# Two sketch rows spread over heads by VectorE, and a task order searched with a price on tiling changes

## The chip, the cores and the metric

One core of a Trainium2 chip. The time of a kernel is the device time of one execution in microseconds (us), taken as the median of several executions. Executions come in a fast and a slow state, and only fast ones are compared; with one core, a run counts as slow when it is over 1.5% above the fastest of its kernel. "The profile" is one traced execution: its span is a little shorter than the timed figure (90.0 of 92.07 us before). TensorE appears as PE (matmuls) and PEld (weight loads), VectorE as DVE, ScalarE as ACT, GpSimd as POOL, SyncE as SP.

## The reference

Polynomial-sketch attention followed by an RWKV channel mix; everything is f32 at the interface.

```python
# q, k, v: [4 batches, 4 heads, 1088, 32];  S1, S2: [8, 32]
def phi(x):                                   # 64 features per token and head
    a = einsum('rd,bhsd->bhsr', S1, x); b = einsum('rd,bhsd->bhsr', S2, x)
    return einsum('bhsi,bhsj->bhsij', a, b).reshape(..., 64)
kv  = einsum('bhsf,bhsd->bhfd', phi(k), v);  z = phi(k).sum(axis=2)
x   = (phi(q) @ kv) / (phi(q) @ z + 1e-6)     # heads side by side: [4, 1088, 128]
# ... x_prev = x one token earlier; xk, xr = mixtures of x and x_prev by mu_k, mu_r
h   = max(xk @ w_k, 0);  v = (h * h) @ w_v    # w_k [128, 1024], w_v [1024, 128]
out = sigmoid(xr @ w_r) * v                   # [4, 1088, 128]
```

## The kernel before

The kernel is a list of tasks with an engine (and a PSUM bank) for each, written by a search that ran beforehand. The list fixes the order of instructions on every engine.

```python
ORDER = """
SS/PE/b0 SM/DVE SC3/ACT SC1/POOL ... KP0_0/PE/b0 KE0_0/ACT ... Z/5 KA0_0_0/PE/b0 ...
"""                                  # [cut] some 580 entries
for t, eng in plan.order(ORDER):
    dummy(t) if eng == "Z" else t["fn"](eng)
```

Names in it: KT/KP/KE/KF/KA are, for a batch's keys, transpose, projection, eviction, outer product and accumulation; KZ to KB fold the result; QT/Q1/.../QX are the same for groups of queries, up to the matmul that makes x; M1 and M2 are the two layers of the channel mix for a tile of 512 tokens (four blocks of 128), RE and SQ its relu and square, RR and SG its gate, FN the last multiply and OD the stores of an output tile.

The sketch rows are repeated over the four heads by the load itself, transposed on TensorE and then masked into block form:

```python
S8 = const.tile([R, 2, H, D], F32)                       # R = 8, H = 4, D = 32
load_k(0, nc.sync)
nc.scalar.dma_start(S8[:, 0], _ap(S1, [[0, H], [1, D]]))  # 32 runs of 128 bytes
nc.scalar.dma_start(S8[:, 1], _ap(S2, [[0, H], [1, D]]))
# ... [cut]
def s_rep():
    p = bank("ss")
    for x in range(2):
        nc.tensor.transpose(p[:, x * R:x * R + R], S8[:, x].rearrange("r h d -> r (h d)"), ident[:R, :R])
```

The key projection consists of short matmuls, two to a group of 128 tokens, each on half of the array (the tiling 128x64). The key accumulation is on quarters (128x32), the channel mix on the whole array (128x128).

```python
def k_proj(b, gi):
    t0, t1 = KG[gi]; p = bank(f"kab_{b}_{gi}")
    for t in range(t0, t1):
        for c in range(2):
            nc.tensor.matmul(p[64*c:64*c+64, (t-t0)*64:(t-t0)*64+64], kT[b][:, t, 64*c:64*c+64],
                             SW[:, 0, :H, :2, :], skip_group_check=True, tile_position=(0, 64*c))
```

Of the kernel before, what the change touches and what calls it, by code (L numbers as in the profile page):

```python
# [13 lines left out]
F32 = mybir.dt.float32  # L14
# [14 lines left out]
SS/PE/b0 SM/DVE SC3/ACT SC1/POOL SF/ACT SC2/POOL Z/2 S4T/PE/b0 KT0_0/DVE S4E/ACT KT0_1/DVE Z/2 KP0_0/PE/b0 KE0_0/ACT  # L29
KP0_1/PE/b1 KF0_0_1/POOL KF0_0_0/DVE KE0_1/ACT KF0_1_0/DVE KF0_1_1/POOL Z/5 KA0_0_0/PE/b0 KA0_0_1/PE WL/POOL  # L30
KA0_1_0/PE QT0_1/DVE KA0_1_1/PE MU/PE/b1 KC0/ACT KZ0/DVE QT0_0/DVE OM/ACT KD0/PE/b0 KG0/PE KW0/ACT KT1_0/DVE Q11/PE/b1
WRP/POOL Q10/PE/b2 KB0/DVE KT1_1/DVE QE1/ACT WRC/POOL KP1_0/PE/b0 QE0/ACT QP1/DVE Q12/PE/b3 QP0/DVE QD1/DVE KE1_0/ACT
QD0/DVE QI1/DVE QI0/DVE QN1/DVE KF1_0_0/POOL QN0/DVE QF1_0/DVE KP1_1/PE/b7 QE2/ACT KF1_0_1/DVE QR1_1/PE/b1 DL3k/DMA
QF0_0/POOL KE1_1/ACT QR1_0/PE/b4 QP2/DVE KA1_0_0/PE/b0 QV1_1/DVE QV1_0/ACT KF1_1_1/DVE KF1_1_0/POOL QR0_0/PE/b2
QD2/DVE QR0_1/PE/b4 QI2/DVE QV0_0/DVE QV0_1/ACT QT1_0/DVE QY0/PE/b4 QX1/PE/b2 QT1_1/DVE KA1_1_0/PE XL0/ACT XP0/ACT
XB0/DVE XF0/POOL XP1/ACT QN2/DVE KZ1/DVE DL3v/DMA KC1/ACT QF2_0/POOL XB1/ACT KD1/PE/b7 XK0/DVE KG1/PE XK1/DVE KW1/ACT
M10_1/PE/b4 M10_3/PE/b0 M10_0/PE/b1 KT2_1/DVE Q13/PE/b5 KB1/ACT QF2_1/POOL RE0_1/ACT DL3q/DMA RE0_3/ACT RE0_0/ACT
M11_2/PE/b4 KT2_0/DVE M11_4/PE/b0 M11_5/PE/b1 QE3/ACT M11_7/PE/b7 M11_6/PE/b2 RE1_4/ACT M11_0/PE/b6 SQ0_0/POOL QP3/DVE
RE1_5/ACT M11_3/PE/b3 RE1_2/DVE M10_4/PE/b0 RE1_0/ACT KP2_0/PE/b1 SQ1_2/POOL QD3/DVE RE1_6/ACT RE1_3/DVE RE0_4/ACT
RE1_7/ACT M20_0/PE/b6 QI3/DVE M10_5/PE/b2 M10_2/PE/b4 M10_7/PE/b0 SQ1_1/ACT QR2_1/PE/b3 QN3/DVE RE0_2/DVE QF3_0/DVE  # L40
QR2_0/PE/b7 RE0_7/ACT SQ0_1/POOL RE0_5/ACT QV2_1/ACT M11_1/PE/b0 QF3_1/DVE RR1/PE/b2 M10_6/PE/b4 RE1_1/ACT M20_1/PE
SG1/ACT RR0/PE/b3 QT2_1/DVE KP2_1/PE/b0 SQ1_0/POOL SQ1_3/ACT RE0_6/ACT QR3_0/PE/b2 KE2_0/ACT QT2_0/DVE QV2_0/ACT
QR3_1/PE/b4 SQ0_3/POOL KE2_1/DVE SQ0_2/ACT Q14/PE/b5 QV3_0/DVE KF2_0_1/POOL QV3_1/ACT KF2_1_1/DVE QY2/PE/b7 M20_2/PE
SG0/ACT M20_3/PE QX3/PE/b4 FN0/DVE KF2_0_0/POOL KT3_0/DVE OD0_0/DMA M21_0/PE/b6 QE4/DVE M21_1/PE XP2/ACT XB3/DVE
KF2_1_0/POOL M21_2/PE KA2_0_0/PE/b1 XB2/ACT XK2/DVE M21_3/PE RR2/PE/b3 XP3/DVE M12_0/PE/b7 M12_1/PE/b2 SG2/ACT
KA2_1_0/PE FN1/DVE XE0/POOL RE2_0/ACT KT3_1/DVE OD1_0/DMA M12_4/PE/b6 RE2_1/ACT M12_5/PE/b3 OD1_1/DMA M12_2/PE/b7
KC2/DVE RE2_4/ACT KZ2/DVE M12_6/PE/b0 RE2_5/DVE KD2/PE/b1 SQ2_0/ACT KG2/PE RE2_6/DVE SQ2_2/POOL M12_7/PE/b3
M12_3/PE/b6 KB2/DVE KP3_1/PE/b2 KW2/ACT QT3_1/DVE RE2_2/ACT Q15/PE/b1 RE2_3/ACT QP4/DVE RE2_7/ACT XL1/DVE Q16/PE/b6
QT3_0/DVE SQ2_1/ACT XF1/POOL QD4/DVE M22_0/PE/b3 QI4/DVE QN4/DVE KP3_0/PE/b7 SQ2_3/ACT XK3/DVE QF4_0/POOL M22_1/PE
KE3_0/DVE M22_2/PE QE5/ACT QF4_1/DVE QE6/ACT KF3_0_1/POOL M22_3/PE KE3_1/ACT QP5/DVE M13_1/PE/b4 KF3_0_0/DVE  # L50
M13_2/PE/b5 QR4_0/PE/b0 RE3_1/ACT KF3_1_0/POOL QD5/DVE FN2/DVE KA3_0_0/PE/b7 RE3_2/ACT QV4_0/ACT QI5/DVE M13_4/PE/b4
OD2_3/DMA KF3_1_1/DVE M13_0/PE/b5 QR4_1/PE/b3 OD2_1/DMA RE3_0/ACT QN5/DVE M13_3/PE/b0 QP6/DVE OD2_2/DMA QF5_0/POOL
QF5_1/DVE KA3_1_0/PE RE3_3/ACT OD2_0/DMA QV4_1/DVE M13_5/PE/b5 SQ3_1/ACT M13_7/PE/b0 SQ3_0/POOL M13_6/PE/b2 QD6/DVE
QR5_0/PE/b3 KZ3/DVE RE3_4/DVE QR5_1/PE/b1 KC3/ACT RE3_6/ACT QI6/DVE KD3/PE/b7 QY4/PE/b4 QN6/DVE QV5_0/ACT KG3/PE
QV5_1/DVE KW3/ACT RR3/PE/b2 RE3_5/ACT KB3/DVE QF6_1/POOL QF6_0/DVE QX5/PE/b1 RE3_7/ACT SQ3_2/ACT SQ3_3/POOL Q17/PE/b0
XP4/DVE XL2/ACT XB4/ACT QR6_1/PE/b6 XB5/DVE QE7/ACT RR4/PE/b5 SG3/ACT QP7/DVE Q18/PE/b7 XP5/ACT XK4/DVE XF2/POOL
M23_0/PE/b2 QD7/DVE SG4/ACT QV6_1/DVE XE1/POOL M14_7/PE/b4 M14_1/PE/b3 QI7/DVE M14_5/PE/b5 RE4_7/DVE M14_4/PE/b6
RE4_1/ACT M23_1/PE QN7/DVE RE4_4/ACT M14_0/PE/b4 RE4_5/DVE QF7_1/POOL M14_3/PE/b3 M23_2/PE RE4_0/ACT QF7_0/DVE
M14_2/PE/b5 SQ4_2/ACT M14_6/PE/b6 RE4_3/DVE SQ4_0/POOL QR6_0/PE/b4 QR7_0/PE/b0 QE8/DVE RE4_2/ACT QV6_0/DVE QR7_1/PE/b3
RE4_6/ACT Q19/PE/b5 QP8/DVE QV7_0/ACT XK5/DVE QY6/PE/b6 M23_3/PE QV7_1/ACT SQ4_1/POOL RR5/PE/b0 QE9/DVE SQ4_3/ACT  # L60
QD8/DVE QX7/PE/b3 FN3/DVE QI8/DVE SG5/ACT OD3_4/DMA QP9/DVE QN8/DVE M24_0/PE/b2 QD9/DVE OD3_3/DMA XL3/DVE XP6/ACT
QI9/DVE M15_1/PE/b0 XP7/DVE QF8_1/POOL OD3_0/DMA M15_3/PE/b1 XB6/ACT M24_1/PE OD3_1/DMA QN9/DVE RE5_3/ACT XB7/DVE
M24_2/PE OD3_2/DMA XE2/POOL RE5_1/ACT M24_3/PE QF9_0/DVE XF3/POOL M15_2/PE/b1 M15_7/PE/b0 QF8_0/POOL FN4/DVE
M15_4/PE/b4 RE5_2/ACT RR7/PE/b5 RE5_7/DVE RE5_4/ACT OD4_3/DMA QR9_1/PE/b2 M15_0/PE/b1 SQ5_1/POOL SG7/ACT XK7/DVE
OD4_1/DMA M15_6/PE/b4 QR8_0/PE/b0 RE5_0/ACT OD4_2/DMA RE5_6/DVE QR8_1/PE/b5 QV9_1/ACT OD4_0/DMA QV8_0/ACT QR9_0/PE/b1
XK6/DVE M15_5/PE/b2 SQ5_3/ACT RR6/PE/b4 QV8_1/DVE SQ5_0/POOL M17_5/PE/b6 M17_6/PE/b0 RE5_5/ACT M17_2/PE/b3 RE7_5/DVE
M17_0/PE/b5 QV9_0/ACT M17_7/PE/b7 RE7_6/DVE M17_3/PE/b2 RE7_2/ACT M17_1/PE/b6 QY8/PE/b1 RE7_3/ACT RE7_7/DVE
M17_4/PE/b3 M16_3/PE/b0 SG6/ACT SQ5_2/POOL RE7_0/DVE M16_5/PE/b2 M25_0/PE/b7 SQ7_1/ACT RE7_1/DVE M25_1/PE M16_6/PE/b5
RE7_4/DVE RE6_5/ACT M16_1/PE/b6 QX9/PE/b4 SQ7_0/ACT RE6_6/DVE SQ7_3/POOL RE6_1/DVE SQ7_2/ACT M25_2/PE XP9/DVE M25_3/PE
XB9/DVE RE6_3/ACT M16_4/PE/b6 XB8/DVE M16_0/PE/b5 M16_7/PE/b3 RE6_4/ACT M16_2/PE/b2 FN5/DVE XE3/POOL M27_0/PE/b0  # L70
RE6_0/ACT SQ6_2/POOL RE6_2/DVE M27_1/PE RE6_7/ACT OD5_1/DMA M27_2/PE XP8/DVE SQ6_0/ACT OD5_3/DMA M27_3/PE OD5_2/DMA
XK8/DVE RR9/PE/b3 SQ6_3/ACT OD5_0/DMA RR8/PE/b2 FN7/DVE SQ6_1/POOL M18_4/PE/b1 M18_2/PE/b5 SG9/ACT M18_5/PE/b7
RE8_4/DVE OD7_3/DMA M18_0/PE/b0 SG8/ACT M18_7/PE/b6 RE8_2/DVE OD7_2/DMA M18_1/PE/b3 RE8_5/ACT M18_6/PE/b1 M18_3/PE/b2
OD7_0/DMA RE8_0/ACT RE8_7/DVE M26_0/PE/b5 OD7_1/DMA SQ8_2/POOL RE8_3/ACT RE8_6/DVE M26_1/PE OD7_4/DMA SQ8_1/ACT
M26_2/PE RE8_1/DVE M26_3/PE XK9/DVE SQ8_0/ACT FN6/DVE M19_5/PE/b4 M19_7/PE/b3 SQ8_3/POOL M19_4/PE/b1 M19_1/PE/b2
RE9_7/DVE RE9_5/ACT M19_2/PE/b6 OD6_2/DMA M19_0/PE/b5 M19_6/PE/b0 RE9_1/ACT RE9_4/DVE M19_3/PE/b7 OD6_0/DMA
M28_0/PE/b4 RE9_0/ACT RE9_6/DVE OD6_3/DMA RE9_3/ACT M28_1/PE RE9_2/DVE OD6_1/DMA SQ9_0/ACT M28_2/PE SQ9_2/DVE M28_3/PE
SQ9_3/ACT SQ9_1/DVE M29_0/PE/b6 FN8/DVE M29_1/PE M29_2/PE OD8_2/ACT OD8_0/DMA M29_3/PE OD8_3/DMA OD8_1/ACT FN9/DVE
OD9_1/ACT OD9_2/ACT OD9_0/ACT
# [3 lines left out]
class Plan:  # L83
# [6 lines left out]
    def add(self, name, cost, fn, deps=(), opens=None, uses=()):  # L90
        uses = list(uses) + ([opens[1]] if opens else [])
        self.tasks[name] = dict(name=name, cost=cost, fn=fn, deps=list(deps), opens=opens, uses=uses)
# [24 lines left out]
def kernel(  # L117
# [14 lines left out]
    nc = tc.nc  # L132
# [26 lines left out]
    S8 = const.tile([R, 2, H, D], F32)  # L159
# [29 lines left out]
    nc.scalar.dma_start(S8[:, 0], _ap(S1, [[0, H], [1, D]]))  # L189
    nc.scalar.dma_start(S8[:, 1], _ap(S2, [[0, H], [1, D]]))  # L190
# [70 lines left out]
    dummy(5)  # L261
# [14 lines left out]

    def s_rep():
        p = bank("ss")
        for x in range(2):
            nc.tensor.transpose(p[:, x * R:x * R + R], S8[:, x].rearrange("r h d -> r (h d)"), ident[:R, :R])  # L280

# [33 lines left out]
    add("SS", {"PE": 0.4}, lambda e: s_rep(), ["Ls"], opens=("p", "ss"))  # L315
# [138 lines left out]
    for b in range(B):  # L454
        prev = []
        for gi, (t0, t1) in enumerate(KG):
            n = t1 - t0
            x = f"{b}_{gi}"
            add("KT" + x, {"DVE": 0.128 + 0.00104 * (n * 128)}, lambda e, b=b, gi=gi: k_trans(b, gi), [f"Lk{b}"] + (["DL3k"] if b == 3 else []) + ([f"KP{b - 2}_{gi}"] if b > 1 else []))
            add("KP" + x, {"PE": 0.102 * n + 0.1}, lambda e, b=b, gi=gi: k_proj(b, gi), ["KT" + x, "SM"], opens=("p", "kab_" + x))  # L460
            add("KE" + x, both(64 * n), lambda e, b=b, gi=gi: k_evac(b, gi, e), uses=["kab_" + x])
            parts = [(0, 2), (2, n)] if n == 4 else [(0, 3), (3, n)]
            kf = []
# [354 lines left out]
```

## Time and profile before

| | before |
|---|---|
| time, median of the first 3 runs | 91.78 us (91.51 to 92.11) |
| span of the profiled run | 90.0 us, mean granted clock 0.985 |
| first key projection starts | 7.66 us |
| last multiply starts, ends | 84.05, 84.61 us |
| last multiply to end of span | 5.43 us |

The prediction below shows most of the page. On it are the mean busy share of the core's DMA engines, in tenths for 40 equal slices of the span, rows on DMA queues (packets, MB, share of 16 engines) and the list of waits (engine, line, waited for: us in total, times, longest).

```profile
DMA  2899999999994010200112000002410002234420
...
q8 instruction: 10, 0.16, 0.8%
```

The first line says that the loads keep the DMA engines nearly full from the second slice of 2.25 us to the twelfth (mean share 0.87 in the second, 1.08 from 4.50 to 27.00 us). The second is a queue that the kernel's text never mentions; the page names its kind, instruction. It made ten transfers of 16 KB in 90 us. The third row to read is in the list of TensorE's waits (engine, line, waited for: us in total, times, longest):

```profile
PE ps_h L616 <- issue: 0.7, 1, 0.7
```

"issue" means that TensorE stood still for 0.66 us while nothing that the profile records held it back. It is one of the larger pauses of TensorE outside the start.

### The profile page before, as it was taken

Reading aid. Unit: us, or ns where it says so; the run is one execution under the profiler, and the core shown is the slowest. Engines: PE = TensorE matmul, PEld = TensorE weight load, DVE = VectorE, ACT = ScalarE, POOL = GpSimd, SP = SyncE. Lnnn points to the kernel's source line nnn. Section 1 sums busy time; section 2 is a strip of 40 time slices with the busy share of each in tenths; the row PEclk is TensorE's granted clock in tenths of the full one; section 3 lists DMA queues with packets and bytes.
Section 4 is the critical chain, followed back from the end, with each engine's and each line's share of the span. In section 5 each row is a group of like instructions: output and inputs, shape, how many; then the busy total and the mean of one; then the engine's idle time right before and its main releaser. Section 6 shows DMA issues by size and latency. Waiting matters only on the chain.

```text
span 90.0 us, 3132 instructions
## 1 busy us (share of the span) xinstructions
PE 78.2 (87%) x1255; PEld 59.0 (66%) x1263; DVE 72.5 (81%) x184; ACT 62.0 (69%) x137; POOL 58.2 (65%) x78
## 2 busy tenths in 40 slices
PE   5669999977799999999999999999999999989300
PEld 3247778845588776689776577868855587869200
DVE  4051878998979889998998699999999999999200
ACT  0621223426879657997899879998999999999000
POOL 6010884866856991578796946989999759790000
PEclk9999999999999999999999999999999999999985
DMA  2899999999994010200112000002410002234420
GB/s 62 290 229 360 235 241 393 194 263 374 254 236 131 6 36 0 66 0 0 32 35 60 7 0 0 0 11 83 112 33 0 7 0 77 74 104 104 118 63 24
DMA packets 8667, 9.71 MB, mean 108 GB/s; under 512 B 715, under 2 KB 7501, under 8 KB 8653
## 3 DMA queue, kind: packets, MB, share of 16 engines
q1 hardware_dynamic: 7468, 8.65, 35.8%
q0 software_dynamic: 416, 0.52, 3.3%
q10 hardware_dynamic: 768, 0.34, 1.3%
q8 instruction: 10, 0.16, 0.8%
q14 instruction: 5, 0.03, 0.1%
HBM read 7.81 MB, written 2.23 MB: 111 GB/s over the span
## 4 chain that ended last, share of the span: by engine, by line
PE 60%; DVE 17%; DMA 7%; issue 4%; ACT 3%; ACTq 1%; SPq 1%; POOL 0%; POOLq 0%
PE ps_o L645 11%; PE ps_h L616 9%; DVE k L626 8%; PE ps_abw L506 8%; PE ps_qtp L551 7%; PE ps_kab L382 6%; PE ps_x L572 4%; PE ps_kv L413 4%; DMA S<-in_S_dram 4%; PE wt L258 4%; DMA out_dram<-osb 3%; DVE XK L585 3%; DVE osb L672 2%; PE ps_kf L443 2%; PE ps_r L657 2%
## 5 line engine op out<-in xcount | busy, mean ns | idle before, releaser
L633 POOL TENSOR_TENSOR k<-k 128x1024 bf16<-128x1024 bf16 (+2 forms) x18 | 28.2, 1587 | 6.9 <-ACT k L624 3.5
L624 ACT ACTIVATE k<-ps_h 128x512 bf16<-128x512 f32 (+3 forms) x51 | 24.4, 549 | 2.6 <-PE ps_h L616 2.4
L635 ACT ACTIVATE k<-k 128x1024 bf16<-128x1024 bf16 (+3 forms) x20 | 19.3, 1003 | 0.1
L616 PE MATMUL ps_h<-XK,wk 128*128 128x512 bf16 (+3 forms) x72 | 18.2, 346 | 1.3 <-issue 0.7
L645 PEld LDWEIGHTS <-k 128*128 128x128 bf16 x272 | 15.8, 98 | 4.5 <-POOL k L633 1.4
L645 PE MATMUL ps_o<-wv,k 128*128 128x128 bf16 x272 | 18.3, 219 | 0.1
L626 DVE TENSOR_SCALAR k<-ps_h 128x512 bf16<-128x512 f32 (+3 forms) x29 | 17.1, 633 | 0.8 <-PE ps_h L616 0.4
L365 POOL TENSOR_TENSOR kp<-ab 128x512 f32<-128x512 f32 (+1 forms) x9 | 10.8, 1219 | 4.8 <-ACT ab L270 4.4
L365 POOL TENSOR_TENSOR qp<-an,wsb 128x512 f32<-128x512 f32 x9 | 9.6, 1071 | 3.7 <-DVE an L537 3.0
L616 PEld LDWEIGHTS <-wk 128*128 128x128 bf16 x80 | 7.6, 115 | 4.8 <-issue 2.0
L551 PE MATMUL ps_qtp<-ident,qp 128*128 128x128 f32 x68 | 9.5, 276 | 0.1
L506 PE MATMUL ps_abw<-SW,qT 128*64 128x96 f32 (+1 forms) x120 | 8.2, 256 | 0.4 <-ACT SW L270 0.4
L551 PEld LDWEIGHTS ps_qtp<-ident,qp 128*128 128x128 f32 x68 | 7.6, 141 | 1.2
L506 PEld LDWEIGHTS ps_abw<-SW,qT 128*64 128x64 f32 (+1 forms) x120 | 6.6, 144 | 2.0 <-ACT k L624 0.9
L585 DVE SCALAR_TENSOR_TENSOR XK<-ps_x,mu,PP 128x512 bf16<-128x512 f32 (+8 forms) x13 | 6.9, 549 | 0.5 <-ACT XB L270 0.5
L258 PE MATMUL wt<-zero 128*128 128x512 f32 (+2 forms) x12 | 6.1, 638 | 1.0 <-DVE one L162 1.0
L672 DVE TENSOR_TENSOR osb<-ps_o,r 128x512 f32<-128x512 f32 (+3 forms) x10 | 6.0, 603 | 1.1 <-PE ps_o L645 1.1
L270 ACT COPY qpT<-ps_qtp 128x512 f32<-128x512 f32 (+1 forms) x12 | 6.2, 539 | 1.0 <-PE ps_qtp L551 0.9
L365 DVE TENSOR_TENSOR kp<-ps_kab,ab 128x512 f32<-128x512 f32 (+1 forms) x7 | 5.0, 714 | 2.1 <-ACT ab L270 2.0
L382 PEld LDWEIGHTS ps_kab<-SW,kT 128*64 128x64 f32 x144 | 5.2, 150 | 1.7 <-ACT S L311 0.7
L663 ACT ACTIVATE r<-ps_r 128x512 f32<-128x512 f32 (+3 forms) x10 | 5.6, 581 | 1.0 <-PE ps_r L658 1.0
L382 PE MATMUL ps_kab<-SW,kT 128*64 128x64 f32 x144 | 6.2, 239 | 0.0
(84 smaller groups left out, 121.4 us busy)
## 6 DMA issues: line engine op xcount, KB each, us to landing
hdk<-in_k_dram SPq DMA_DIRECT2D x4, 544.0 KB
hdq<-in_q_dram SPq DMA_DIRECT2D x4, 544.0 KB
out_dram<-osb SPq DMA_DIRECT2D x27, 64.0 KB
vt<-in_v_dram SPq DMA_DIRECT2D x4, 288.0 KB
vt<-in_v_dram SPq DMA_DIRECT2D x4, 256.0 KB
out_dram<-osb ACTq DMA_DIRECT2D x5, 64.0 KB
wk<-in_moe_w_k_dram POOLq DMA_DIRECT2D x1, 256.0 KB, 7.1
wv<-in_moe_w_v_dram POOLq DMA_DIRECT2D x1, 256.0 KB, 10.1
```

The source lines that it names most:

```text
L258: nc.tensor.matmul(wt[:, :m * P], zero[:], _ap(zero[:], [[0, m], [1, P]]), skip_group_check=True)
L365: eng.tensor_mul(o.rearrange("p t h i j -> p (t h) i j"), _ap(a_, [[sa, y], [1, R], [0, R]]), _ap(b_, [[sb, y], [0, R], [1, R]]))
L382: nc.tensor.matmul(p[64 * c:64 * c + 64, (t - t0) * 64:(t - t0) * 64 + 64], kT[b][:, t, 64 * c:64 * c + 64], SW[:, 0, :H, :2, :], skip_gro ...
L506: nc.tensor.matmul(p[lo:hi, t * 96:t * 96 + 96], qT[:, s + lo:s + hi], SW[:, (s + lo) // S, g % 2:g % 2 + H].rearrange("p h x r -> p (h x ...
L551: nc.tensor.transpose(p[:, t * P:t * P + P], qp[g][:, t, 2 * pair:2 * pair + 2].rearrange("p h i j -> p (h i j)"), ident[:])
L585: nc.vector.scalar_tensor_tensor(XK[:, b * S + s:b * S + s + m], tiles[f"x_{g}"][:, c0:c0 + m], mu_k, PP[:, b * XW + s:b * XW + s + m], op ...
L616: nc.tensor.matmul(h[:, :n * P], wkc[:, c // 4, c % 4], XK[:, F0[g] * P:(F0[g] + n) * P])
L624: nc.scalar.activation(o, i, RELU)
L626: nc.vector.tensor_scalar(o, i, 0.0, None, op0=mybir.AluOpType.max)
L633: (nc.vector if eng == "DVE" else nc.gpsimd).tensor_mul(k2[:, :, :n * P], k1[:, :, :n * P], k1[:, :, :n * P])
L635: nc.scalar.activation(k2[:, :, :n * P], k1[:, :, :n * P], mybir.ActivationFunctionType.Square)
L645: nc.tensor.matmul(o[:, t * P:t * P + P], k2s[g, j][:, c, t * P:t * P + P], wv[:, w * j + c, :], start=(j == 0 and c == 0 and t == 0), sto ...
```

## The change

It has two intents. Load the sketch rows once (8 runs of 128 bytes for each) and repeat them over heads by a VectorE copy, to start sooner. And search the order again, with a price on each change of TensorE's tiling, so that tasks of one tiling stand together. The old order changes the tiling 54 times, the new one 44 times.

```diff
 ORDER = """
-SS/PE/b0 SM/DVE SC3/ACT ... (every line of the order is new)
+SH/DVE SS/PE/b0 SM/DVE SF/ACT SC1/POOL KT0_1/DVE ... Z/1 KP0_1/PE/b1 KP0_0/PE/b0 ...
-    S8 = const.tile([R, 2, H, D], F32)
+    S8 = const.tile([R, 2, D], F32)
+    S8h = const.tile([R, 2, H, D], F32)
-    nc.scalar.dma_start(S8[:, 0], _ap(S1, [[0, H], [1, D]]))
+    nc.scalar.dma_start(S8[:, 0], S1)                        # and S2 likewise
+    def s_heads():
+        for x in range(2):
+            nc.vector.tensor_copy(S8h[:, x], _ap(S8[:, x], [[0, H], [1, D]]))
-    dummy(5)
+    dummy(7)
-    WHOLE = 3        # query groups projected with whole tiles
+    WHOLE = 2
     # [cut] buffers: qp 2 -> 3, qpT 2 -> 3, relu 8 -> 10, square 7 -> 8, gate 3 -> 4
     # [cut] cost figures and a tiling mode on the tasks, used by the search only
```

## The prediction

Passages that no trace or run of this case shows are cut from the text below, each cut marked. -0.9 - 0.7 + 0.5 = -1.1, and -0.2 more, takes 91.78 to 90.5 us. But the -0.9 leans on the case of sketch rows that land at 4.2 us ("First projection"). The passages that led to 4.2 are cut, and no trace showed it: take it as an assumption of the author. The 0.09 us of a tiling change is read off the trace rows there. DMA engines were busy for 0.90 of the time from 1.68 to 5.24 us, while the rows were on their way.

> **What bounds the kernel now.** I read the page first for busy shares, then the chain that ended last, then the start in order of time, then busy time by stage. The page's first lines:
>
> ```profile
> PE 78.2 (87%) x1255; PEld 59.0 (66%) x1263; DVE 72.5 (81%) x184; ACT 62.0 (69%) x137; POOL 58.2 (65%) x78
> PE   5669999977799999999999999999999999989300
> DVE  4051878998979889998998699999999999999200
> PE 60%; DVE 17%; DMA 7%; issue 4%; ACT 3%; ACTq 1%; SPq 1%; POOL 0%; POOLq 0%
> ```
>
> TensorE (PE) and VectorE (DVE) are both nearly full, and TensorE carries 60% of the chain that ended last. There is no single bound, so I asked which engine holds which stretch. Ahead of 62 us the chain is almost all TensorE, passing through small hand-offs; then it changes engine:
>
> ```profile
> 1.37 3.82 DMA S<-in_S_dram
> 5.24 0.27 PE ps_ss L280
> 7.73 1.68 PE ps_kab L382 x36
> ...
> 61.93 0.59 DVE qp L365
> 62.53 0.60 DVE osb L672
> ...
> 66.33 3.46 DVE k L626 x6
> ...
> 84.05 0.56 DVE osb L672
> ```
>
> In the first three lines the reader is to see a start-up of 5.2 us that waits for 4 KB of sketch rows, and only then the first key projection, at 7.7 us. From 61.9 us VectorE works without a gap worth naming, 0.58 to 0.60 us for each tile of 512 columns (3.46 us for 6). Busy time by stage (stretch, its length, then busy us of PE, PEld, DVE, ACT, POOL):
>
> ```profile
> 7.66:13.38 5.72, 5.65 (x141) 4.58 (x140) 3.67 (x8) 1.24 (x5) 3.75 (x6) 1.00 1.08 277
> 13.38:22.00 8.62, 7.20 (x170) 5.90 (x170) 7.97 (x27) 3.99 (x14) 5.81 (x9) 1.00 1.09 299
> 22.00:42.00 20.00, 19.09 (x363) 14.84 (x365) 18.12 (x49) 15.90 (x44) 13.67 (x18) 1.00 0.36 93
> 42.00:63.13 21.13, 20.86 (x340) 15.71 (x342) 19.45 (x54) 18.66 (x38) 17.17 (x21) 1.00 0.11 25
> 63.13:84.60 21.47, 20.31 (x241) 15.30 (x243) 20.67 (x37) 19.99 (x35) 15.78 (x11) 1.00 0.24 56
> ```
>
> VectorE idles 2.05, 0.65, 1.88, 1.68 and 0.80 us in these five stretches, 7.1 us in all. That idle time, more than any engine's total, is what a better order can take. The last 5.4 us of the span hold the final stores only and do not change.
>
> [...] in a stretch where nothing waits:
>
> ```profile
> 48.23 0.22 PE L658 MATMUL ps_r<-wr_p,XB 128*128 128x128 bf16 x1
> 48.38 0.25 PE L657 MATMUL ps_r<-wr_c,XB 128*64 128x128 bf16 x2
> 48.46 0.23 PE L658 MATMUL ps_r<-wr_p,XB 128*64 128x128 bf16 x2
> 48.61 0.23 PE L657 MATMUL ps_r<-wr_c,XB 128*128 128x128 bf16 x1
> 48.68 0.22 PE L658 MATMUL ps_r<-wr_p,XB 128*128 128x128 bf16 x1
> 48.74 0.22 PE L657 MATMUL ps_r<-wr_c,XB 128*128 128x128 bf16 x1
> 48.79 0.22 PE L658 MATMUL ps_r<-wr_p,XB 128*128 128x128 bf16 x1
> ```
>
> The first number is the start. From one matmul to the next inside one tiling it is 0.05 to 0.07 us; across the change (48.23 to 48.38) it is 0.15. A change costs some 0.09 us. [...] the second sketch load was issued from 1.37 to 1.68 us and its transpose started at 5.24 us, 3.6 us later. [...] key and value loads of half a MB each fill the engines by then[...]. [...] a 128x32 VectorE copy from SBUF took 0.23 us here.
>
> **The change part by part.**
>
> Start. The two loads become 8 runs of 128 bytes each in place of 32. [...] if queueing is set by the big loads ahead and not by its own runs, it stays at 5.2. Added: two VectorE copies on 8 partitions (about 0.3 us for the pair, estimated from the 0.23), ahead of both transposes (0.27 each, overlapping). The mask product therefore ends at landing + 0.9 us, against landing + 0.6 before (5.20 to 5.79). Then the order helps: the new one projects the second key group first, into a bank that the S4 transpose did not use, and so needn't wait for ScalarE's read of that bank (PE waited 0.65 us for it, first projection at 7.66, 1.87 us after the mask). It needs only two VectorE transposes of 0.4 to 0.5 us. First projection: landing + 1.85, so 6.1 us (landing 4.2) to 7.05 (landing 5.2), or 0.6 to 1.6 us earlier. Part is given back: VectorE now takes 3 of the 4 key outer products in batch 0 (two before), an eviction of 320 columns (0.45 us) and both query transposes (1.03 + 0.56) ahead of the key mask, where only the long transpose stood before. I get the key mask and copy finished at projection start + 5.6 us against + 4.84 before, but with more of the later VectorE work done. Net 0.4 to 1.4 us; I take **-0.9**.
>
> Tiling changes. Counting task groups along PE's order I find 54 changes before and 44 after: 10 x 0.09 = 0.9 us. Query group 2 goes from whole to half tiles: 8 whole matmuls took 1.06 us in the chain, 16 halves 0.81, so 0.25 more. All lie ahead of 60 us (two changes remain behind that in either kernel). PE has 60% of the chain, so I credit 0.6 x 1.15 = **-0.7**.
>
> Shift of work. VectorE 157 to 165 tasks, ScalarE 134 to 129, GpSimd 49 to 47. By row durations less the roughly 0.1 us that successive ones overlap, VectorE gains some 1.2 us (5 more small copies of keys' state, 7 more relus, 1 more square, 1 outer product, against 5 fewer x evictions and 1 fewer query eviction), ScalarE about 0.5, GpSimd loses nearly 3 (its 1024-column square takes 1.9 us, its outer products 1.07). About half of VectorE's 1.2 falls where it idled: **+0.5**. Behind the fifth output tile (at 62.5 us before) VectorE has 32 tasks for 36, ScalarE 35 for 40, PE 22 wide first-layer matmuls for 28. That makes the VectorE-bound end about 2.5 us shorter, but the work only moves ahead, into the middle with its 3.6 us of VectorE idle time (22 to 63 us). So it is a condition for the gain, no gain of its own.
>
> Buffers: a third buffer for query features and their transposes, two more for relu and one for square tiles, one for the gate. They let the order run further ahead; no wait in the page has a buffer as its largest cause. Nothing credited. Dummy matmuls: 9 units to 11, 0.2 us each, in waits; nothing.
>
> Sum: -0.9 - 0.7 + 0.5 = -1.1; a little more, -0.2, for an order whose load times fit better. 91.78 - 1.3 gives **90.5 us**.
>
> **The rivals.** (a) The start gain is hidden. After 14 us VectorE is 92% busy and the loads are still running (DMA share about 1.09 to 22 us); if the second batch's loads, not VectorE, set the pace, an earlier start is only waited out. Against it: up to 22 us no engine's idle time in the list of waits is put down to those loads. Then about 91.3. (b) VectorE becomes the bound of the middle too: it has 1.2 us more to do, and a hand-off that misses costs 0.3 to 0.7. Against it: 7.1 us of idle time. Then 91.8 to 92.5. (c) The searched order works as a whole: most of VectorE's idle time in the middle goes, and the shorter end is kept. For it: GpSimd, slowest per element, is relieved by 3 us. Then 88.8 to 89.5.
>
> **Range and chances.** The main course 90 to 91.2 (half), (a) or (b) 91.2 to 92.3 (a quarter), (c) below 90 (a quarter). 2% is 1.84 us, so faster needs 89.9. Range 89.0 to 91.9. Faster 0.28, within 2% 0.68, slower 0.04.
>
> **What would show it.** Right: first key projection at 6.1 to 7.0 us, a shorter DMA piece at the chain's head; PE total shorter by about a microsecond [...]; fifth output tile at 63 to 64 us, later than before, and under 20 us from there to the last output. Wrong: sketch rows still landing at 5.2 us; VectorE still idling over 3 us between 22 and 63 us (then (b)); a fifth output tile after 65 us, or an end as long as before.

## More of the kernel before

All loads of the first three batches are given to SyncE's queue at once, in the order in which they are needed. The loads of batch 3 are given out later, into the buffers of batch 1 (tasks DL3k, DL3v, DL3q):

```python
load_k(0, nc.sync); load_v(0, nc.sync); load_q(0, nc.sync)   # [cut] other work between these
load_k(1, nc.sync); nc.sync.dma_start(wr_f[:], moe_w_r)
load_v(1, nc.sync); load_q(1, nc.sync)
load_k(2, nc.sync); load_v(2, nc.sync); load_q(2, nc.sync)   # 544 KB each
```

## The result, and the profile after

| | before | after |
|---|---|---|
| time, median of 4 runs | 91.94 us (91.51 to 96.93) | 96.45 us (96.26 to 99.35) |
| ratio of fast runs | | 1.05 (1.0441 to 1.0559): slower |
| span of the profiled run | 90.0 us | 94.4 us |
| mean granted clock | 0.985 | 0.962 |
| first key projection starts | 7.66 us | 7.34 us |
| last multiply ends | 84.61 us | 87.56 us |
| last multiply to end of span | 5.43 us | 6.81 us |

A ratio, here and below, is the mean time of one kernel's fast runs over the mean time of the other's fast runs of the same rounds, so it is not quite the ratio of the medians quoted. The range behind it is a 95% interval.

The span grew by 4.34 us: 2.95 us up to the end of the last multiply and 1.38 us after it. The page of the changed kernel:

```profile
span 94.4 us, 3137 instructions
...
PE 79.9 (85%) x1268; PEld 60.0 (64%) x1273; DVE 72.8 (77%) x194; ACT 62.5 (66%) x131; POOL 55.3 (59%) x76
...
PE   5979999676499999999999999999899999998000
...
PEclk9999999999958999999999999999999999999965
...
PE 63%; ACT 11%; DVE 10%; DMA 4%; issue 3%; ACTq 1%; DVEq 0%
```

Read the two strips together. TensorE has a hole in the eleventh slice (the 4), and its granted clock falls to 5 tenths in the twelfth slice and 8 in the thirteenth; the strip shows it as full everywhere else before the end. The clock strip before has no such place (9 in every slice but the last two). The waits of TensorE name the hole, and the chain places it (start, duration, what):

```profile
PE ps_kab L388 <- issue: 2.1, 1, 2.1
```

```profile
1.39 3.67 DMA S<-in_S_dram
5.08 0.23 DVE S8h L280
...
7.41 1.77 PE ps_kab L388 x36
...
21.45 0.59 PE ps_x L578 x16
22.04 0.73 PE ps_kab L388 x19
22.77 2.13 issue
24.90 0.22 PE ps_kab L388
...
87.00 0.56 DVE osb L678
```

TensorE stops for 2.13 us inside one task: after 19 of the 20 matmuls of a key projection, all of which have the same inputs ready. No data can be missing for the twentieth. The chain of the kernel before has its small pause at almost the same end time, also inside a task, a first-layer group:

```profile
23.63 0.56 PE ps_h L616 x4
24.19 0.66 issue
24.85 0.57 PE ps_h L616 x4
```

Busy time by stage after (stretch, length, busy us of PE, PEld, DVE, ACT, POOL with instruction counts, granted clock, DMA share, GB/s):

```profile
22.00:23.00 1.00, 0.77 (x26) 0.64 (x20) 0.80 (x4) 0.85 (x4) 0.20 (x1) 1.00 0.49 132
23.00:24.00 1.00, 0.00 (x0) 0.00 (x0) 0.00 (x0) 0.29 (x1) 1.00 (x4) 1.00 0.82 229
24.00:25.00 1.00, 0.10 (x1) 0.00 (x0) 0.00 (x0) 0.00 (x0) 0.52 (x1) 1.00 1.10 237
26.00:27.00 1.00, 1.00 (x18) 0.88 (x15) 0.56 (x2) 0.80 (x5) 0.00 (x0) 0.50 1.01 371
```

While TensorE stands, VectorE and ScalarE run dry too. Then the clock is 0.50: the trace gives it as 0.5 from 25.69 to 29.11 us, 3.41 us in all.

**The place in TensorE's own list.** Counting TensorE's records in the trace (weight loads, matmuls and the few semaphore records, in order of time) gives this, with the second transfer of the instruction queue from the same trace:

```
                                        before          after
records in all                          2548            2565
record 448 (us)                         17.89           18.93
record 704 (us)                         23.92           22.55
next record after 704 (us)              24.85           24.90
second instruction transfer (us)        22.20..23.30    22.43..23.51
first-layer matmuls in records 448-704  7               0
```

Records are counted from 0. The transfers are of 16 KB, and there are ten of them, as many as the records 192, 448, 704 and so on in steps of 256 that TensorE passes. (The step is the distance from 448 to 704, the two records behind which traces of the experiments stop, four and nine of them.) What one transfer brings is called a block here. In both kernels TensorE stops at record 704, and in both it goes on 1.39 to 1.55 us after the second transfer ended. So the reading is: TensorE had run out of instructions. The new order gets through the 256 records ahead of that place in 3.6 us instead of 6.0, as it has put short matmuls of one tiling together. Here are TensorE's rows there (start, busy us), first after, then before:

```profile
20.07 0.65 PE L419 MATMUL ps_kv<-kp,vt 128*32 128x64 f32 x32 [0.65 <-DVE kp L371]
...
20.60 0.74 PE L419 MATMUL ps_kv<-kp,vt 128*32 128x64 f32 x40
...
21.38 0.66 PE L578 MATMUL ps_x<-qpT,kvS 64*32 64x256 f32 x16
21.97 0.80 PE L388 MATMUL ps_kab<-SW,kT 128*64 128x64 f32 x19
```

```profile
22.34 0.36 PE L616 MATMUL ps_h<-XK,wk 128*128 128x128 bf16 x3
22.63 1.01 PE L506 MATMUL ps_abw<-SW,qT 128*64 128x96 f32 x16
23.57 0.63 PE L616 MATMUL ps_h<-XK,wk 128*128 128x256 bf16 x4
```

In the new order 72 + 18 accumulations, 16 matmuls for x and 19 key projections lie back to back. In the old one, wider query projections and first-layer matmuls lie among them.

**The end.** What follows the last multiply, before and then after:

```profile
84.60:90.03 5.43, 0.00 (x0) 0.00 (x0) 0.00 (x1) 0.00 (x0) 0.00 (x0) 0.75 0.27 73
```

```profile
87.56:94.37 6.81, 0.00 (x0) 0.00 (x0) 0.00 (x0) 0.00 (x0) 0.00 (x0) 0.72 0.34 80
```

The last multiplies started at 75.06, 79.11, 82.65 and 84.05 us before, at 80.49, 83.08, 85.55 and 87.00 after. Tile 7 has five stores, which SyncE issues at 0.54 us each. Before, it issued them from 75.77 to 78.65 us, after, from 83.79 to 86.68 us, and tile 8's two behind them up to 87.63 us, when tile 9 was ready. The last packet of the stores that ScalarE issues (tile 9 among them) ended 3.96 us after the last multiply before, and 5.34 us after it in the new order.

### The profile page after: what moved, and what is told of

The parts are those of the page before. It is cut to its first block, busy times and chain, and to the rows that moved or that the text cites. A ratio compares the mean times of both kernels' runs of the same rounds, so it can differ in the third digit from the quotient of the medians.

```text
span 94.4 us, 3137 instructions
## 1 busy us (share of the span) xinstructions
PE 79.9 (85%) x1268; PEld 60.0 (64%) x1273; DVE 72.8 (77%) x194; ACT 62.5 (66%) x131; POOL 55.3 (59%) x76
## 4 chain that ended last, share of the span: by engine, by line
PE 63%; ACT 11%; DVE 10%; DMA 4%; issue 3%; ACTq 1%; DVEq 0%
PE ps_o L651 13%; PE ps_h L622 13%; PE ps_kv L419 5%; PE ps_kab L388 5%; PE ps_qtp L557 5%; PE ps_abw L512 5%; ACT k L630 4%; PE ps_x L578 4%; PE wt L259 4%; DMA S<-in_S_dram 4%; PE ps_r L663 2%; DVE qT L495 2%; ACT k L641 2%; PE ps_r L664 2%; ACT PP L587 2%
## 5 line engine op out<-in xcount | busy, mean ns | idle before, releaser
L639 POOL TENSOR_TENSOR k<-k 128x1024 bf16<-128x1024 bf16 (+2 forms) x16 | 26.3, 1654 | 6.0 <-DVE k L632 3.1
L632 DVE TENSOR_SCALAR k<-ps_h 128x512 bf16<-128x512 f32 (+3 forms) x36 | 20.8, 604 | 2.4 <-PE ps_h L622 1.2
L630 ACT ACTIVATE k<-ps_h 128x512 bf16<-128x512 f32 (+3 forms) x44 | 21.8, 550 | 0.3
L622 PE MATMUL ps_h<-XK,wk 128*128 128x512 bf16 (+3 forms) x75 | 20.6, 351 | 0.6 <-DVE XK L591 0.2
L651 PEld LDWEIGHTS <-k 128*128 128x128 bf16 x272 | 16.8, 98 | 3.6 <-issue 0.9
L371 POOL TENSOR_TENSOR kp<-ab 128x512 f32<-128x512 f32 (+1 forms) x7 | 8.8, 1257 | 11.0 <-ACT ab L271 8.2
L371 POOL TENSOR_TENSOR qp<-an,wsb 128x512 f32<-128x512 f32 x10 | 10.6, 1068 | 1.5 <-DVE an L543 1.5
L259 PE MATMUL wt<-zero 128*128 128x512 f32 (+3 forms) x14 | 7.5, 654 | 1.0 <-DVE one L163 1.0
L587 ACT ACTIVATE PP<-ps_x,omu 128x512 f32<-128x512 f32 (+6 forms) x9 | 4.7, 543 | 4.3 <-PE ps_x L578 4.3
L419 PE MATMUL ps_kv<-kp,vt 128*32 128x64 f32 x288 | 5.7, 222 | 0.8 <-DVE kp L371 0.6
```

What stands on the lines that cost most here:

```text
L259: nc.tensor.matmul(wt[:, :m * P], zero[:], _ap(zero[:], [[0, m], [1, P]]), skip_group_check=True)
L371: eng.tensor_mul(o.rearrange("p t h i j -> p (t h) i j"), _ap(a_, [[sa, y], [1, R], [0, R]]), _ap(b_, [[sb, y], [0, R], [1, R]]))
L419: nc.tensor.matmul(kv[32 * h:32 * h + 32, :64], vt[b][:, h, T, :], kp[:, t, h].rearrange("p i j -> p (i j)"), start=(T == 0), stop=(T == 8 ...
L622: nc.tensor.matmul(h[:, :n * P], wkc[:, c // 4, c % 4], XK[:, F0[g] * P:(F0[g] + n) * P])
L630: nc.scalar.activation(o, i, RELU)
L632: nc.vector.tensor_scalar(o, i, 0.0, None, op0=mybir.AluOpType.max)
```

## The experiments

Theory **F**: TensorE runs out of instructions at record 704, since the second block arrives late behind the loads and the new order eats the first blocks faster; the stop then costs the clock as well. Rival **D**: the stop is a data wait that the profile does not name (a bank, a semaphore, the load of batch 2), or the new order is simply worse later on. Twelve kernels ran. Labels that begin with a_ are edits of the kernel after, those with b_ of the kernel before; shift and warm are edits of the kernel after. They ran on three chips, on each of them together with runs of the kernel before, and each ratio is to the runs on the same chip.

### shift: 7 dummy matmuls' worth of wide work replaced by 8 short matmuls (in the kernel after)

```diff
-KF0_0_1/DVE Z/7 KA0_0_0/PE/b2
+KF0_0_1/DVE Z/-8 KA0_0_0/PE/b2      # Z/-8: eight matmuls of one column
```

> The changed kernel with 8 one-column matmuls in place of the 7 dummy units ahead of the first key accumulation: 24 more TensorE records early, nothing else. Theory F (TensorE runs out of instructions: both kernels stop at their record 704 and go on at 24.9 us): the stop stays near record 704, so it comes 6 float32 matmuls earlier in the program, after 7 or 8 of the 20 records of the third batch's second key projection instead of 19, and ends at 24.5 to 25.3 us; half clock after it again, time 96.4 +- 0.7 us. Rival W (that matmul waits for data or a bank): the stop stays at the 20th record.

Measured: 99.25 us (96.23 to 99.69), its profile slow. With the short dummies the clock stayed at half until 22.3 us (there the trace has its first clock event; a matmul of the key projection takes 0.31 us before it and 0.22 behind). TensorE came to record 704 only at 28.14 us and did not stop there. For the index test this is inconclusive: two things changed at once. The second transfer came at 22.79 us, just as TensorE reached record 448 (22.81). The later transfers, when no loads crowd the DMA engines, lie in the same way: in the kernel before they start at 33.25, 37.94 and 44.39 us, and TensorE reaches records 960, 1216 and 1472 at 32.51, 37.84 and 43.77. So a block seems to be asked for one block ahead of its use. In the kernels before and after, the second transfer started 4.3 and 3.5 us after record 448.

### warm: two wide dummies ahead of the projection in which TensorE stopped (after)

```diff
         p = bank(f"kab_{b}_{gi}")
+        if (b, gi) == (2, 1):
+            for _ in range(2):
+                nc.tensor.matmul(p[:], zero[:], _ap(zero[:], [[0, 4], [1, P]]), skip_group_check=True)
```

> The changed kernel with two 512-column dummy matmuls (1.7 us) just ahead of the projection in which it stops. Theory F: the instructions still come at 24.9 us, so the stop shrinks from 2.1 to about 0.4 us and the work behind it starts no later, but TensorE stays busy and no half-clock stretch follows: 1.0 to 1.8 us less than the changed kernel (94.6 to 95.4 us). Rival (the half clock costs nothing because other engines hold the middle): within 0.4 us of 96.4, or slower by the 1.7 us of dummies.

Measured: 96.04 us (95.41 to 97.64), ratio 1.0421 (1.0376 to 1.0467). TensorE in its trace:

```profile
20.30 1.98 PE L388 MATMUL ps_kab<-zero 128*128 128x512 f32 x4
22.21 0.69 PE L391 MATMUL ps_kab<-SW,kT 128*64 128x64 f32 x16
24.75 0.34 PE L391 MATMUL ps_kab<-SW,kT 128*64 128x64 f32 x4 [1.85 <-issue]
```

The stop is now after 16 of the 20 projections, no longer after 19: again exactly record 704, as the dummies put more records in front. A data wait would have stayed at its task. TensorE resumed at 24.75 us although it was 1.7 us ahead at record 448 (17.27 us against 18.93; full clock from 4.06 us), so that lead gained nothing. The stop was 1.85 us and no half clock followed (9 tenths in every slice but the last two). From the resumption to the end of the last multiply it took 61.6 us, against 62.7 in the kernel after: by this the half clock cost about 1.1 us. The same stretch takes 61.96 us in a_gate below, which makes it 0.7. The fast runs' mean was 0.6 us under that of the kernel after (95.83 against 96.39, taken at different times), not the 1.0 to 1.8 that I expected.

### a_gate: values and queries of batch 2 loaded later (after)

```diff
-    hdq = [const.tile([P, 2 * U, D], F32, name=f"hdq{b}") for b in range(B - 1)]
+    hdq = [const.tile([P, 2 * U, D], F32, name=f"hdq{b}") for b in range(2)]   # vt likewise; batch 2 uses batch 0's
-    load_v(2, nc.sync)
-    load_q(2, nc.sync)
-    add("DL3v", ..., lambda e: load_v(3, nc.sync), ...)
+    add("DL3v", ..., lambda e: (load_v(2, nc.sync), load_q(2, nc.sync), load_v(3, nc.sync)), ...)
```

> The changed kernel with the loads of batch 2's values and queries put into batch 1's buffers, so that they start after 21 us: about 1.1 MB less in the DMA queues ahead of it. Theory F with the queue as the cause of the late block: the second 16 KB instruction transfer starts before 21 us instead of 22.4, the stop is under 0.5 us or gone, no half-clock stretch; 92 to 93.5 us. If instructions come late for another reason than the loads: stop as before, 96.4 or more. If the order itself is bad: stop gone but still over 94.5 us.

Measured: 93.4 us (92.5 to 94.34), ratio to before 1.0102 (1.0042 to 1.0162), against 1.05 for the change as it was. The second transfer ran at 20.00 to 20.98 us. The chain at the old place of the stop:

```profile
21.42 0.59 PE ps_x L577 x16
22.02 0.73 PE ps_kab L387 x20
22.75 0.34 PE ps_kf L442 x2
...
83.92 0.56 DVE osb L677
```

All 20 projections run through, TensorE goes straight on, and the clock stays full (1.00 in each us from 22 to 30). The order on TensorE is the same as in the kernel after; 1.1 MB left the load queue. The last multiply ends at 84.48 us: 3.08 us ahead of the kernel after (stop and half clock), and level with the kernel before (84.61, its own stop of 0.66 us included). What remains is the end:

```profile
84.48:91.30 6.82, 0.00 (x0) 0.00 (x0) 0.00 (x0) 0.00 (x0) 0.00 (x0) 0.75 0.33 78
```

### b_gate: the same edit in the kernel before

The diff is that of a_gate.

> The same gating of loads in the kernel before: its stop of 0.66 to 0.9 us at record 704 goes. Theory F: 91.0 to 91.6 us, a little faster than before. Rival (the stop in the kernel before is not of the loads): 91.8 or slower.

Measured: 94.43 us (93.18 to 95.03), ratio 1.0168 (1.009 to 1.0247), its profile slow. The transfer came at 19.98 us and the stop was gone. But a miss of mine took its place, as the old order wants batch 2's queries sooner (VectorE, idle before it in brackets):

```profile
31.02 1.04 DVE L488 STREAM_TRANSPOSE qT<-hdq 128x832 f32<-128x832 f32 x1 [2.96 <-DMA hdq<-in_q_dram]
```

The stop went in this order as well, but the expected gain (91.0 to 91.6 us) did not come: the fast runs are 0.9 to 2.5% slower. The 2.96 us are the only cause in sight.

### a_nost7: a_gate without the stores of tile 7 (wrong result)

```diff
-OD7_3/DMA ... OD7_1/DMA ... OD7_4/DMA ... OD7_0/DMA ... OD7_2/DMA
```

> The gated changed kernel without the five stores of output tile 7 (the output is wrong on purpose). Its last multiply came at 83.92 us, as early as in the kernel before (84.05), but the span ended 6.8 us after it instead of 5.4. Theory T (the stores of tiles 7 and 8 are still in the DMA queues when tile 9 is stored, since the last three tiles come closer together): the end behind the last multiply shrinks to 5.0 to 5.6 us. Rival (something else at the end, such as the closing barrier): it stays at 6.6 to 7.0 us.

Measured: 92.49 us in one run (state unknown). After the last multiply:

```profile
85.32:90.61 5.29, 0.00 (x0) 0.00 (x0) 0.00 (x1) 0.00 (x0) 0.00 (x0) 0.82 0.26 73
```

With tile 7's five issues out of SyncE's way the end is 5.29 us, that of the kernel before (5.43). So the 1.4 us at the end come from tile 7's stores, close ahead of the last ones. Whether it is SyncE's time to issue them or their bytes in the queues, this run does not separate.

### b_tail: one of the last three stores from SyncE rather than ScalarE (before)

```diff
-OD9_1/ACT OD9_2/ACT OD9_0/ACT
+OD9_1/ACT OD9_2/DMA OD9_0/ACT
```

> The kernel before with the middle one of the last three stores moved from ScalarE's queue to SyncE's. Theory T, that the end is a matter of the stores' queue: 0.3 to 1.0 us less than before (about 91.3). Rival (the end is set by fixed latency): within 0.2 us of before.

Measured: 92.95 us, ratio 1.0044 (0.9985 to 1.0102); the end was 5.34 us against 5.43. The expected gain did not come. In the old order SyncE has issued its last store by 84.2 us, ahead of the last multiply's end, and the end is not bound by who issues the last three.

### b_gate2: only batch 2's values late (before)

```diff
-    load_v(2, nc.sync)
+    add("DL3v", ..., lambda e: (load_v(2, nc.sync), load_v(3, nc.sync)), ...)   # [cut] vt's buffers as in a_gate
```

> The kernel before with only batch 2's values loaded late (their first use is at 34.7 us), the queries as before. Theory F: the second instruction transfer starts about 1.8 us earlier, the stop of 0.66 us at record 704 goes, 0.3 to 0.8 us less than before. In the first gating the late query load cost VectorE 3.0 us; here it shouldn't wait.

Measured: 92.15 us (91.35 to 92.69), ratio 0.9996 (0.9937 to 1.0055). The transfer came at 20.57 us and the stop was gone, as F says, but the time did not move: in the profiled run the start was later (first projection at 7.93 us rather than 7.66), and its last multiply ended at 84.59 us, no earlier than before. A miss on the time.

A start that differs by this much needs no edit. With the same start-up code the first projection lies at 6.75, 7.07, 7.66, 7.74 and 7.93 us in five traces of the old order, and between 6.24 and 7.67 in five of the new. Differences of a few tenths there say nothing.

### b_heavy: one more load of 544 KB at the end of the queue (before)

```diff
+    more = const.tile([P, 2 * U, D], F32)
+    nc.sync.dma_start(more[:], q[2].rearrange("h (a t) d -> (h a) t d", a=32))
```

> The kernel before with one more load of 544 KB (never read) in SyncE's queue behind batch 2's queries. Theory F: the instruction block comes 1.5 to 2 us later, the stop at record 704 grows from 0.66 to 2.2 to 2.7 us, half clock may follow; 1.5 to 3.5 us slower than before. Rival (a stop that has nothing to do with the loads): the stop stays at 0.66 us and the time within 0.5 us.

Measured: 93.44 us (92.19 to 96.11); fast runs 1.0027 (0.9953 to 1.0102). The profiled execution (94.2 us, slow) has the transfer at 24.41 us, later than any other, and in its chain:

```profile
25.27 1.64 issue
26.92 0.57 PE ps_h L618 x4
```

That is record 704 again, later and longer than before. The data of this load are used by nothing. The granted clock stayed full (mean 0.984 over the run, 0.985 before). In the two fast runs, which have no profile, no loss is to be seen, so the effect on time, expected as 1.5 to 3.5 us, is not shown.

The start of the second transfer against what waits in the load queue, over all traces: 19.26 to 20.91 us with 1.1 MB less (four traces), 20.57 and 21.62 with 0.56 MB less, 22.20 to 23.89 as it is (seven), 24.41 with 0.56 MB more.

### b_news: the sketch part of the change alone (before)

```diff
-    nc.scalar.dma_start(S8[:, 0], _ap(S1, [[0, H], [1, D]]))   # and S2; [cut] the tile S8h and its two transposes
+    nc.scalar.dma_start(S8[:, 0], S1)
+            nc.vector.tensor_copy(S8h[:, x], _ap(S8[:, x], [[0, H], [1, D]]))
```

> The kernel before with the sketch rows loaded once and spread by VectorE, that part of the change alone. In the changed kernel the first rows came early (2.99 us) but the second only at 5.08, and the copy and the step to TensorE took 0.3 us more: within 0.5 us of before, no gain. Rival (this part is where the changed kernel lost): slower by over 1 us.

Measured: 93.78 us (93.42 to 94.47), ratio 1.0172 (1.0076 to 1.0268): slower, against my expectation. The first projection started at 6.90 us, 0.76 us earlier, which is within the spread of the old start. And then:

```profile
24.85 1.64 issue
26.49 0.57 PE ps_h L619 x4
```

The transfer came at 23.89 us here, so the stop grew from 0.66 to 1.64 us. Why it came later with the same bytes ahead of it is not shown. On the chip of this run half of the load queue had landed at 11.35 us (11.39 in b_s2), in the five other traces with these loads at 10.4 to 10.9 us; but the kernel before has no trace from that chip. So whether the edit itself costs time stays open.

### b_s2: the load of S2 put first in SyncE's queue (before)

```diff
+    nc.sync.dma_start(S8[:, 1], _ap(S2, [[0, H], [1, D]]))
     load_k(0, nc.sync)
-    nc.scalar.dma_start(S8[:, 1], _ap(S2, [[0, H], [1, D]]))
```

> The kernel before with the second sketch load issued by SyncE ahead of the first key load, instead of second on ScalarE's queue. If the second rows are late because they queue behind the key load: both are there by 3.5 us, the second transpose runs at 3.5 to 4 us instead of 5.2, the first key projection 0.7 to 1.3 us earlier, and 0.3 to 1.0 us less than before in the end. Rival (the keys themselves, or other waits, take the place): the start gains under 0.3 us and the time is within 0.3 us.

Measured: 94.63 us (93.7 to 95.43), ratio 1.0217 (1.0133 to 1.03); its profile was slow. The second transpose ran at 3.60 us, as expected of rows that no longer queue behind the key load. The first projection came at 5.93 us, 1.7 us earlier than before and outside the spread of the old start, and the kernel got slower. Its chain, and one stretch of its stages:

```profile
23.59 2.46 issue
26.06 0.94 PE ps_h L616 x4
```

```profile
31.00:32.00 1.00, 1.00 (x16) 0.80 (x15) 0.45 (x3) 0.96 (x4) 0.89 (x1) 0.50 0.01 4
```

TensorE reached record 704 sooner and waited longer there, for a transfer that came at 23.48 us. The half clock after this stop lasted from 25.47 to 32.29 us, 6.83 us. A run is called slow by its time alone, so a long stop with half clock may be what made this one slow; but the ratio is from fast runs alone.

### b_best: b_s2 and b_gate2 together (before)

The diff is the sum of the two.

> The same with batch 2's values loaded late, so that the earlier start does not only lengthen TensorE's stop at record 704. Theory F: 0.3 to 0.8 us less than with the early sketch rows alone, 0.8 to 1.6 us less than before.

Measured: **90.66 us** (90.09 to 92.18), ratio 0.9825 (0.9761 to 0.989): it beats both kernels. Its chain at the place:

```profile
23.43 0.55 issue
23.98 0.57 PE ps_h L616 x4
...
83.17 0.56 DVE osb L672
```

With the second block at 21.62 us, 1.9 us earlier than in b_s2, the early start (first projection at 5.71 us) is worth something: the stop is 0.55 us, the clock stays full (9 tenths in every slice but the last, mean 0.985), and the last multiply starts 0.88 us ahead of before. Either part alone gave nothing, or a loss. And even this kernel still waits for instructions, at record 704 and one block earlier. Behind record 448 (16.11 us) TensorE stands until 17.16, 1.30 us after the first transfer ended; its list of waits has

```profile
PE ps_kv L413 <- issue: 0.8, 1, 0.8
```

### a_best: a_gate, S2 first, and two of tile 7's stores from GpSimd (after)

```diff
-OD7_0/DMA M29_0/PE/b5 ... OD7_2/DMA
+OD7_0/POOL M29_0/PE/b5 ... OD7_2/POOL
# and the edits of a_gate and b_s2
```

> The changed kernel with the loads gated (93.4 us, no stop), the second sketch load first on SyncE, and two of the five stores of tile 7 issued from GpSimd, idle at that time. Theory: the start comes 0.7 to 1.2 us earlier, the end behind the last multiply falls from 6.8 to 5.4 to 6.2 us: 91 to 92 us, level with before or up to 1% faster. If the changed order is bad in itself: still over 93 us.

Measured: 92.1 us (90.92 to 94.28), ratio of its fast runs 0.9914 (0.9828 to 1.0001). The last multiply ends at 82.98 us and the end takes 5.82 us rather than 6.82. The second transfer came at 19.26 us, but TensorE was early too, and a pause of 0.52 us is left at record 704. With its three faults mended as far as that, the new order is about level with the old kernel, and not ahead of the old order mended in the same way.

**All traces together.** Nine of the fourteen traces have a stop behind record 704, and in all nine the next record starts 1.29 to 1.55 us after the end of the second transfer, though these ends lie anywhere from 20.22 to 25.50 us. In the other five the next record starts 1.47 us or more after the transfer, and TensorE does not stop there (the gap is at most 0.16 us). In four traces (b_heavy, b_news, b_s2, b_best) it stands behind record 448 as well, for 0.2 to 1.05 us, and goes on 1.30 to 1.44 us after the first transfer. That is the test by index that shift was meant to be: another block edge, other tasks, the same wait.

**What stays open.** That TensorE waited for instructions is inferred, as the profile calls it "issue" only: five things speak for it (record 704 in every kernel that stopped; the same time from the transfer's end to the resumption; the stops at record 448; the stop moved from task to task by added records; the stop taken away by a shorter load queue with nothing else moved on TensorE). What sets the start of the second transfer is shown only so far: it comes near record 448 where the load queue has run dry, and later the longer that queue is.

## Why the prediction was wrong

**Predicted 90.5 us, within 89.0 to 91.9; it was 96.45.** None of the rivals held it, as all of them were about engines and data.

- **"Tiling changes ... -0.7" failed, and this is the step that mattered.** The count, 54 to 44, is right; the cost of 0.09 us was read off one change and not tested. But it was taken as a pure saving, as if the instructions were always there. Short matmuls of one tiling one after the other use up instructions faster: 256 records in 3.6 us against 6.0. The next block came at the same time in both kernels, so TensorE resumed at 24.90 us against 24.85, with ten changes of tiling saved and nothing won. It resumed with less done, too: the 704 records before it held no first-layer matmul, where the old order had seven. From there to the end of the last multiply it took 62.66 us against 59.76; 0.7 to 1.1 us of the difference is the half clock, the rest work still to do. Without the stop (a_gate) the new order's last multiply ends at 84.48 us, against 84.59 in the old order without its stop (b_gate2): the order itself was neutral.
- **The pause was in the views I had read.** "issue" had 4% in the chain's summary that the prediction shows, and the waits named the 0.66 us pause. I did not ask what it was. The change turned 0.66 us into 2.13.
- **The half clock was not among the ways it could go wrong.** It cost about 0.7 to 1.1 us of the 3.1 by which a_gate's last multiply is earlier.
- **"The last 5.4 us ... do not change" failed:** 6.81 us, for the stores of tile 7 queued on SyncE (5.29 us without them).
- **"Start ... -0.9" failed in size, and its gain is not shown.** The sketch rows came at 5.08 us, not at the assumed 4.2, and the first projection started at 7.34 us, 0.3 earlier; I had said 6.1 to 7.05. But both vary from execution to execution. The second rows were copied at 4.2 to 5.4 us over six traces with the new load, and were transposed at 4.3 to 5.5 us over five with the old one, so neither the saving nor its absence can be read from one pair. That they queue behind the key load, which I had named as the alternative, is shown by b_s2 (3.60 us). The sum was off as well: a gain of 0.6 to 1.6 us less a give-back of 0.76 is not 0.4 to 1.4; more than half of the give-back was set against later work without a figure. The key mask came at 12.95 us against 12.31, so by 13 us no gain was left in this pair. And b_s2 shows that an earlier start, which lies outside the spread, would have been lost at record 704. Rival (a), an early start that is waited out, was thus right in kind, for instructions rather than for batch 2's data.
- **"Shift of work ... +0.5" and rival (b).** VectorE idles 5.1 us from 22 to 42 us, which by the prediction's list would mean (b). But in a_gate, with the same division of work, it idles 2.06 us there, about as much as before (1.88). VectorE's load did not become the bound; it starved with TensorE.
- **Checks.** The fifth output tile came at 67.0 us (62.44 before), and "after 65 us" was on the list of what would be wrong. From there to the last output it took 20.6 us, against 22.2 before and "under 20" as expected: the shorter end was partly there, on top of a delay. TensorE's busy total grew from 78.2 to 79.9 us rather than shrinking, half clock included.

## What to carry to other kernels

A long list of instructions is itself loaded, by the reading above (ten transfers of 16 KB for some 2550 records of TensorE): where the trace has an "issue" pause inside a run of equal instructions, count the engine's records up to it and look at the instruction queue's transfers, above all while big loads fill the DMA engines (share 1.08 here). Then an earlier start or a denser order may do no more than lengthen the pause (0.66 us before, 2.46 in b_s2, 2.13 after); half clock followed the pauses of 2.13 and 2.46 us, for 3.41 and 6.83 us. The cure here was to keep loads that are not needed yet out of the queue (b_best: 90.66 us, where its early start alone lost). And look at the spacing of the last output tiles: five stores close ahead of the last ones made the end 1.4 us longer, though no engine had more to do.

## What the traces show of instruction blocks, the clock and tiling

- TensorE stopped at record 704 for 0.5 to 2.46 us in nine traces. The traces fit two blocks held at a time: the first transfer comes at 15.35 us in the kernel before, while TensorE is between records 192 (11.16 us) and 448 (17.89), and TensorE stands behind record 704 until the second has come. No run tests the number.
- Stops of 2.13 and 2.46 us were followed by half clock (3.41 us after, twice that, 6.83, in b_s2), stops of 1.64 and 1.85 us were not. The changes of the clock lie whole multiples of 3.41 us apart: 78.51 us (23 times) before, 17.06, 3.41 and 61.44 us (5, 1 and 18 times) after. If that grid is laid over the stops, the idle time inside one step is 2.13 us (after) and 1.87 (b_s2) where half clock followed, and 1.64 in warm, b_heavy and b_news where it did not. So the phase seems to count; no run tests it.
- Grouping by tiling is a trade here: across one change of tiling the next matmul started after 0.15 us, against 0.05 to 0.07 inside a tiling, but ten changes fewer won nothing (84.48 us against 84.61 to the last multiply, with the stop removed).
